# The last batch's gated products in equal 1024-wide pieces, with two two-bank value tiles

## The chip, the core and the metric

The kernel runs on one core of a Trainium2 chip. The metric is the device time of one execution in microseconds. [...] Each engine takes its instructions in the order in which the program lists them, and semaphores order the engines among each other.

## The reference

Per batch an induced attention block (32 inducing vectors attend to 12416 tokens, and the tokens attend to the result), and then a gated feed-forward layer over all tokens:

```python
def mab(q, kv):
    s = scale * (q @ kv.transpose(0, 2, 1))
    s = s - s.max(-1, keepdims=True)
    a = np.exp(s)
    a /= a.sum(-1, keepdims=True) + 1e-09
    return a @ kv
h = mab(I, x)            # B=4, m=32, C=128
attn = mab(x, h)         # N=12416 tokens a batch
...
gate = 1.0 / (1.0 + np.exp(-(x @ w_gate)))   # x: 49664 x 128, w_gate: 128 x 1536
val = x @ w_val
return (gate * val @ w_out).astype(np.float32)
```

## The kernel before

Four batches follow each other; a batch has 97 chunks of 128 tokens, and six groups of 16 chunks plus one chunk left over. Since the second attention's output is a (weights, 32 wide) times h, the kernel folds h into the two weight matrices (`hwt`), so that the feed-forward layer multiplies the 32-wide transposed attention weights `a2r` by `hwt` directly. Hidden columns come in 12 strips of 128 (`NJ`), tokens in blocks of four chunks, 512 tokens (`BC`). There are 97 blocks, the last of them made of the four leftover chunks.

The main loop goes through *steps*. Before, a block has eight: strips are taken two, one, two, one and so on, and a step of two strips is 1024 wide, a step of one 512. `product(t)` (L1033) puts on PE the value matmuls of step t into `v_ps` and the gate matmuls of step t + 2 into `g_ps` (both by `hidden_mm`, L998), and on DVE the product u = (t + 1) * v (L1042). `gate(t)` (L1023) puts the tanh that empties `g_ps` into an SBUF tile on ACT (L1029); the sigmoid is a half of 1 + tanh of a half. `project` (L1063) puts the projections on PE (L1073): four 128 x 128 matmuls a strip, which add u times w_out into the one-bank tile `acc`; after a block's last strip ACT copies `acc` out (L1091) and SP stores it. In the very last block the result stands in two tiles, of which ACT copies one and DVE the other (L1084, L1086).

PSUM's eight banks before: gate tiles of two banks and of one (`g2`, `g1`), value tiles of two banks and of one (`v2`, `v1`), `acc` one, and `m` one for everything else. Each is a single buffer, so a refill of a gate tile waits for the tanh that reads it, and a refill of a value tile for the product that reads it. Before, a wide product also waits, by a dependency added by hand, for the gate refill of step t + 2.

The attention of other groups is worked in between. A *slot* is two steps of the loop; `at(slot, make, late)` plans a piece, and `beside` issues it after the product of that slot's first or second step. `plan_stage2` plans a group's second attention: two slots of score matmuls into `m` (L609), a copy of the scores to SBUF by ACT (L643), lowering by the row maximum on POOL, exp on ACT (L669), sums, inverse and spreading on POOL, and a transposing DMA on SP that makes `a2r`. In the last batch, whose first slot is called o here (slot 288, step 576), groups 2 to 5 are scored from slots o + 4, o + 20, o + 36 and o + 56 on; the scores lie in one SBUF buffer, `sc`. Slot 12 of the last batch, o + 12, begins with step 600 and block 75; 22 blocks follow from there, with block 96.

The order around the change is the order in which this code is written: no scheduler moves an instruction, and `project` is called at the end of every second step, with room for three or four strips.

Of the kernel before, what the change touches and what calls it, by code (L numbers as in the profile page):

```python
# [19 lines left out]
BC = 4  # L20
# [6 lines left out]
def kernel(  # L27
# [34 lines left out]

    ps = ctx.enter_context(tc.tile_pool(name="ps", bufs=1, space=bass.MemoryType.PSUM))

    xv = x.rearrange("b (p j) c -> b p j c", p=P)
    ov = out.rearrange("(b p j) c -> b p j c", b=B, p=P)
# [19 lines left out]
    def x_transpose_dma(b, s):  # L88
        c0, n = groups[s]
        if s == 0 and b > 1:  # L90
            c0, n = 0, n + NLO
        xT_tile(b)
        nc.sync.dma_start(
            xT[b][:, c0 : c0 + n, :],
            xn[b][:, c0 : c0 + n, :].rearrange("p j c -> p (j c)"),
            transpose=True,
        )

    xT_tile(0)
    idle = xT[0][:, NCH - 4 : NCH, :]  # L100
# [614 lines left out]
        for j in range(n):  # L715
            a2[(b, c + j)] = (a2r, j)

    def plan_stage2(b, c, score, take, weigh, far=None, soon=False, lag=None):
# [6 lines left out]
        def room():  # L725
            st["sc"] = s2p.tile([P, GC + NLO, m], F32, tag="sc", name="sc", bufs=1)
# [36 lines left out]
        if far is not None:  # L763
            at(far, one)
            at(far + 1, lambda: s2_take(st["sc"], GC, NLO, st["s2"]))
        at(score, lambda: half(0, False))
        at(score + 1, lambda: half(GC // 2, not soon))
        if soon:
            for k in range(2):
                at(weigh - 1 + k, lambda k=k: s2_shift(GC, st["s2"], *st["hl"], which=(k,)))  # L770
        else:
            at(take, keep, late=True)
            at(take if lag is None else lag, lower, late=lag is None)
# [218 lines left out]
    for i in range(len(blocks)):  # L992
        for j in range(0, NJ, 3):
            steps.append(dict(block=i, j0=j, cnt=2))
            steps.append(dict(block=i, j0=j + 2, cnt=1))
    NST = len(steps)

    def hidden_mm(st, what, halves=False):  # L998
        pt = ps.tile([P, st["cnt"], 512], F32, tag=f"{what}{st['cnt']}", name=f"{what}_ps")
        pieces, col = [], 0  # L1000
        for b, c, nb in blocks[st["block"]]:
            pieces += [(k, b, c, nb, col) for k in range(st["cnt"])]
            col += nb * P
        if not halves:
            pieces.sort(key=lambda p: p[0])
        for k, b, c, nb, col in pieces:
            j = st["j0"] + k
            r = 32 * (j % 2 + (2 if what == "v" else 0))
            a2r, o = a2[(b, c)]
            st[what + "end"] = nc.tensor.matmul(  # L1010
                pt[:, k, col : col + nb * P],
                hw[b][r : r + 32, j // 2, :],
                a2r[r : r + 32, o : o + nb, :].rearrange("p j t -> p (j t)"),
                start=True,
                stop=True,
            )
        st[what] = pt

    def gate_fill(t):
        if t < NST:  # L1020
            hidden_mm(steps[t], "g", t == 0)

    def gate(t):  # L1023
        if t < NST:
            st = steps[t]
            st["t"] = tp.tile([P, st["cnt"], 512], F16, tag=f"t{st['cnt']}", name="t16")
            cuts = [0, 512] if t else [0, 256, 512]
            for c, e in zip(cuts, cuts[1:]):
                st["tanh"] = nc.scalar.activation(  # L1029
                    out=st["t"][:, :, c:e], in_=st["g"][:, :, c:e], func=AF.Tanh, scale=0.5  # L1030
                )

    def product(t):  # L1033
        st = steps[t]
        hidden_mm(st, "v")
        if t == 0:
            keep_on(3, "acc")
        gate_fill(t + 2)
        st["u"] = up.tile([P, st["cnt"], 512], F16, tag=f"u{st['cnt']}", name="u16")
        cuts = [0, 512] if 0 < t < NST - 1 else [0, 256, 512]  # L1040
        for c, e in zip(cuts, cuts[1:]):
            u = nc.vector.scalar_tensor_tensor(  # L1042
                out=st["u"][:, :, c:e],
                in0=st["t"][:, :, c:e],
                scalar=1.0,
                in1=st["v"][:, :, c:e],
                op0=ALU.add,
                op1=ALU.mult,
            )
            if t == 0 and c == 0:  # L1050
                turn_b()
        if st["cnt"] == 2 and 4 <= t < NST - 2:

            tc.declare_no_dep(u.ins, st["tanh"].ins, reason="the gate fill of t + 2 waits for it")
            tc.add_manual_dep(
                u.ins, steps[t + 2]["gend"].ins.name, AFTER, reason="tanh, gate fill, product"
            )

    acc = [None]
# [3 lines left out]
    def project(upto, now, room):  # L1063
        while queue and queue[-1][0] < upto and room > 0:
            t, k = queue.pop()
            st = steps[t]
            j = st["j0"] + k
            if j == 0:
                acc[0] = [ps.tile([P, BC, C], F32, tag="acc", name="acc_ps")]
                if st["block"] == len(blocks) - 1:  # L1070
                    acc[0].append(ps.tile([P, BC, C], F32, tag="m", name="acc_ps"))
            for i in range(BC):
                nc.tensor.matmul(  # L1073
                    acc[0][(i // 2) % len(acc[0])][:, i, :],
                    st["u"][:, k, ts(i, P)],
                    wo16[:, NI * (j % 2) + j // 2, :],
                    start=(j == 0 and i in ((0, 2) if len(acc[0]) > 1 else (0,))),
                    stop=(j == NJ - 1),
                    skip_group_check=True,
                )  # L1080
            room -= 1
            if t == NST - 1:
                o32 = op.tile([P, BC, C], F32, tag="o32")
                nc.scalar.mul(out=o32[:, 0:2], in_=acc[0][0][:, 0:2], mul=0.5)  # L1084
                nc.scalar.dma_start(ov0[:, 0, 0:2, :], o32[:, 0:2])
                nc.vector.tensor_scalar_mul(out=o32[:, 2:4], in0=acc[0][1][:, 2:4], scalar1=0.5)  # L1086
                nc.sync.dma_start(ov0[:, 0, 2:4, :], o32[:, 2:4])
            elif j == NJ - 1:
                block = blocks[st["block"]]
                o32 = op.tile([P, BC, C], F32, tag="o32")  # L1090
                nc.scalar.mul(out=o32[:], in_=acc[0][0][:], mul=0.5)  # L1091
                b, c, nb = block[0]
                nc.sync.dma_start(ov[b, :, c : c + BC, :], o32[:])
                if now < NST:
                    return


    base = [first_step[(b, 0)] // 2 for b in range(B)]
    for b in range(B):
# [6 lines left out]
        for s in range(3 if b == 0 else 2, NG - 1):  # L1106
            k = o + 16 * s - 28
            if b == 0 and s == 4:
                k += 1
                plan_stage2(b, groups[s][0], k, k + 1, k + 13)  # L1110
                continue
            lag = k + 4 if b and more and s == 3 else None
            plan_stage2(b, groups[s][0], k, k + 2, k + (14 if more else 10), lag=lag)
        late = 2 if more and b else 0
        plan_stage2(b, groups[NG - 1][0], o + 56, o + 58, o + 66, far=o + 52 + late)
        if not more:
            continue
        if b == 0:
            parts = {
                2: (23, (29, 29, 29)),  # L1120
# [55 lines left out]
    for t in range(2):  # L1176
        gate_fill(t)
        gate(t)
    for t in range(NST):
        product(t)  # L1180
        gate(t + 2)
        if t % 2 == 0:
# [1 line left out]
        else:  # L1184
            beside(t // 2, True)
            project(t - 1, t, 3 if waiting(t - 1) <= 3 else 4)
    assert not plan
    project(NST, NST, 10**6)

# [29 lines left out]
```

## Time and profile before

| what | before |
|---|---|
| median of 3 runs | 717.21 us (717.18 to 717.42) |
| the profiled execution | 717.26 us |
| its span, first to last instruction | 715.3 us |
| granted TensorE clock in it | 0.999 |
| DVE busy in the span | 697.8 us (98%) |
| ACT busy | 674.2 us (94%) |
| PE busy | 648.1 us (91%) |
| POOL busy | 446.6 us (62%) |

The table's busy times are unions of records. On DVE, ACT and PE a record of one instruction overlaps the start of the next, so that a busy share near 100% doesn't say by itself that no more instructions would fit; what an instruction costs its engine is the distance from its start to the next one's. In a timeline row, the first number is the start in us from the span's start, the second the length that the row covers, "x12" the number of instructions merged into it, and a bracket the idle time before it and what released it.

### The profile page before, as it was taken

What the parts mean: (1) busy time and instruction counts of PE and PEld (TensorE: products, weight loads), DVE (VectorE), ACT (ScalarE), POOL (GpSimd) and SP (SyncE); (2) the same over time, 40 slices, a digit from 0 to 9 for tenths busy, and PEclk for the clock granted to TensorE, in tenths of its full rate; (3) what the DMA queues carried; (4) which work ended last, traced back from release to release, by engine and by line L of the source; (5) the groups of instructions that cost most, each with busy time, mean ns of one, the idle gap of its engine ahead of it and who ended that gap; (6) DMA issues with size and microseconds to landing.
All of it is one profiled execution on the core that took longest, in us unless ns stands there. A gap on an engine that the chain in (4) does not pass through costs nothing.

```text
span 715.3 us, 21657 instructions
## 1 busy us (share of the span) xinstructions
PE 648.1 (91%) x8475; PEld 393.2 (55%) x8475; DVE 697.8 (98%) x850; ACT 674.2 (94%) x1018; POOL 446.6 (62%) x780
## 2 busy tenths in 40 slices
PE   7999899998999999999998989999989889898887
PEld 4555465555555555655555556555555555555555
DVE  4899999999999999999999999999999999999997
ACT  4799999999999999999999999999999999999996
POOL 4468863887558978668656887587737546535100
PEclk9999999999999999999999999999999999999999
DMA  8979964254583264155484142221222123121201
GB/s 172 178 132 187 139 134 92 75 119 88 110 164 75 67 118 108 58 116 108 92 158 106 49 76 77 60 61 51 57 76 64 42 75 61 45 60 46 76 32 47
DMA packets 116855, 65.24 MB, mean 91 GB/s; under 512 B 99952, under 2 KB 101136, under 8 KB 116752
## 3 DMA queue, kind: packets, MB, share of 16 engines
q1 hardware_dynamic: 112064, 49.83, 31.4%
q0 software_dynamic: 4416, 13.90, 10.9%
q8 instruction: 66, 1.08, 0.6%
q14 instruction: 37, 0.30, 0.1%
q10 hardware_dynamic: 272, 0.13, 0.1%
HBM read 27.80 MB, written 25.43 MB: 74 GB/s over the span
## 4 chain that ended last, share of the span: by engine, by line
DVE 49%; issue 20%; PE 16%; ACT 11%; DMA 2%; DVEq 1%; POOL 0%; ACTq 0%; POOLq 0%
DVE u L1042 47%; ACT t L1029 10%; PE acc_ps L1073 7%; PE v_ps L1010 6%; DMA xn<-in_x_dram 2%; PE hp_ps L281 1%; DVE nm L233 1%; DVEq L1042 1%; PE g_ps L1010 1%; POOL xn L82 0%; ACT a1T L246 0%; ACT hwt L468 0%; PE s_ps L609 0%; DVE nmx L620 0%; ACT o L1091 0%
## 5 line engine op out<-in xcount | busy, mean ns | idle before, releaser
L1042 DVE SCALAR_TENSOR_TENSOR u<-t,v_ps 128x512 f16<-128x512 f16 (+1 forms) x778 | 674.9, 945 | 1.1 <-ACT t L1029 0.6
L1029 ACT ACTIVATE t<-g_ps 128x512 f16<-128x512 f32 (+1 forms) x777 | 592.3, 820 | 20.6 <-ACT t L1029 12.7
L1010 PE MATMUL v_ps<-a2r,hwt 32*128 32x512 f16 (+1 forms) x1188 | 293.9, 371 | 55.3 <-DVE u L1042 53.9
L1073 PE MATMUL acc_ps<-wo,u 128*128 128x128 f16 x4656 | 327.6, 220 | 0.2
L1073 PEld LDWEIGHTS <-u 128*128 128x128 f16 x4656 | 261.0, 98 | 88.4 <-issue 87.5
L1010 PE MATMUL g_ps<-a2r,hwt 32*128 32x512 f16 (+1 forms) x1188 | 297.0, 377 | 0.0
L1010 PEld LDWEIGHTS <-hwt 32*128 32x128 f16 x2424 | 92.7, 91 | 185.8 <-issue 140.4
L699 POOL TENSOR_TENSOR a2n<-e,rs 128x2048 f16<-128x2048 f16 (+3 forms) x25 | 86.8, 3474 | 5.0 <-DVE rs L688 2.1
L677 POOL TENSOR_TENSOR sum<-e 128x256 f32<-128x256 f16 (+1 forms) x23 | 15.4, 669 | 97.6 <-ACT e L669 97.6
L438 POOL TENSOR_TENSOR near<-sme,minus 128x16 f32<-128x16 f32 (+1 forms) x22 | 65.2, 2963 | 1.6
L1091 ACT ACTIVATE o<-acc_ps 128x512 f32<-128x512 f32 x96 | 58.2, 607 | 0.0
L653 POOL TENSOR_TENSOR rise<-sc 128x256 f32<-128x256 f32 (+1 forms) x22 | 16.3, 739 | 43.4 <-ACT sc L643 43.3
L654 POOL TENSOR_SCALAR rise<-rise 128x256 f32<-128x256 f32 (+6 forms) x110 | 30.1, 273 | 9.6
L657 POOL TENSOR_TENSOR top<-top,rise 128x128 f32<-128x128 f32 (+3 forms) x88 | 28.3, 321 | 7.3
L677 POOL TENSOR_TENSOR sum<-sum 128x128 f32<-128x128 f32 (+3 forms) x92 | 28.3, 308 | 7.2
L653 POOL TENSOR_TENSOR rise<-top 128x128 f32<-128x128 f32 (+3 forms) x88 | 27.2, 309 | 6.9
L660 POOL TENSOR_TENSOR sc<-sc,top 128x512 f32<-128x512 f32 (+1 forms) x22 | 23.9, 1086 | 1.7
L609 PEld LDWEIGHTS <-xT 128*128 128x128 f16 x388 | 13.1, 96 | 11.7 <-issue 11.3
L82 POOL DMA_DIRECT2D xn<-in_x_dram x25 | 14.9, 602 | 6.5 <-DMA xn<-in_x_dram 5.6
L609 PE MATMUL s_ps<-hT,xT 128*128 128x32 f16 x388 | 18.2, 178 | 0.1
L657 POOL TENSOR_TENSOR top<-sc,rise 128x256 f32<-128x256 f32 (+1 forms) x22 | 16.2, 737 | 1.8
L360 POOL TENSOR_TENSOR xT<-xT 128x512 f32<-128x512 f32 (+2 forms) x13 | 12.4, 954 | 4.2 <-ACT xT L343 3.6
(160 smaller groups left out, 282.4 us busy)
## 6 DMA issues: line engine op xcount, KB each, us to landing
out_dram<-o SPq DMA_DIRECT2D x96, 256.0 KB, 2.3
xn<-in_x_dram POOLq DMA_DIRECT2D x19, 512.0 KB, 8.0
xn<-in_x_dram POOLq DMA_DIRECT2D x4, 544.0 KB, 6.4
a2r<-a2n SPq DMA_TRANSPOSE x29, 4.4
xn<-in_x_dram POOLq DMA_DIRECT2D x1, 384.0 KB, 14.8
wg<-in_moe_w_gate_dram POOLq DMA_DIRECT2D x1, 384.0 KB, 16.3
wv<-in_moe_w_val_dram POOLq DMA_DIRECT2D x1, 384.0 KB, 16.6
wo<-in_moe_w_out_dram POOLq DMA_DIRECT2D x1, 384.0 KB, 16.1
```

The costliest lines, as they stand in the source:

```text
L438: nc.gpsimd.tensor_tensor(out=near, in0=x, in1=minus, op=ALU.pow)
L609: nc.tensor.matmul(s2[:, j, :], xT[b][:, c + j, :], hT16[b][:], start=(j == 0), stop=whole and j == j1 - 1, skip_group_check=True,)
L653: nc.gpsimd.tensor_tensor(out=r, in0=far, in1=near, op=ALU.subtract)
L654: nc.gpsimd.tensor_scalar(out=r, in0=r, scalar1=BIG, scalar2=0.0, op0=ALU.min, op1=ALU.max)
L657: nc.gpsimd.tensor_tensor(out=top[:, 0:n, 0:w], in0=near, in1=r, op=ALU.add)
L677: nc.gpsimd.tensor_tensor(out=d[:, 0:n, :], in0=src[:, :, 0:w], in1=src[:, :, w : 2 * w], op=ALU.add)
L699: eng.tensor_tensor(out=a2n[:, 0:n, :, :], in0=e.unsqueeze(2).to_broadcast((P, n, 4, m)), in1=rs.unsqueeze(2).unsqueeze(3).to_broadcast((P ...
L1010: st[what + "end"] = nc.tensor.matmul(pt[:, k, col : col + nb * P], hw[b][r : r + 32, j // 2, :], a2r[r : r + 32, o : o + nb, :].rearrange ...
L1029: st["tanh"] = nc.scalar.activation(out=st["t"][:, :, c:e], in_=st["g"][:, :, c:e], func=AF.Tanh, scale=0.5)
L1042: u = nc.vector.scalar_tensor_tensor(out=st["u"][:, :, c:e], in0=st["t"][:, :, c:e], scalar=1.0, in1=st["v"][:, :, c:e], op0=ALU.add, op1= ...
L1073: nc.tensor.matmul(acc[0][(i // 2) % len(acc[0])][:, i, :], st["u"][:, k, ts(i, P)], wo16[:, NI * (j % 2) + j // 2, :], start=(j == 0 and ...
L1091: nc.scalar.mul(out=o32[:], in_=acc[0][0][:], mul=0.5)
```

## The change

Up to slot 12 of the last batch the loop keeps its steps. From there on:

- Every product is 1024 wide: a block has six steps of two strips. The gates are still made in eight pieces of two strips and one (`gates`), six strips and four pieces to three steps.
- PSUM is laid out anew: the pool with `v1` and `m` is closed, and its two banks become a second two-bank value tile `vw`; value refills take `v2` and `vw` in turn.
- The tanh results go to the space of batch 2's token tile `xn[2]`, four sets of six strips, since a product now reads strips that two tanh instructions made.
- `project` runs after every step, with room for two or three strips, and not in the step after a block's copy.
- `m` is gone there, so the last batch's scores are made ahead, from slots o - 8, o, o + 4 and o + 8 on, and copied aside into batch 2's transposed token tile `xT[2]`. Lowering, exp and the rest keep their slots.
- The very last block has one `acc` tile; its last product is cut at 384 of 512 tokens, and its last eight projections are ordered to match.
- Apart from the region: eight transposing DMAs of token groups (batches 2 and 3, groups 1 to 4) are issued in two pieces of eight chunks.

```diff
+    gates = steps
+    T0 = first_step[(B - 1, 0)] + 2 * 12
+    steps = gates[:T0]
+    for i in range(gates[T0]["block"], len(blocks)):
+        for j in range(0, NJ, 2):
+            steps.append(dict(block=i, j0=j, cnt=2, bank="vw" if j % 4 else "v2"))
...
     def product(t):
...
-        gate_fill(t + 2)
+        if t < T0:
+            gate_fill(t + 2)
+        else:
+            st["t"] = wide_t((t - T0) // 3, st["j0"], 2)
+            k = T0 + (t - T0) // 3 * 4
+            gate_fill(k + (2, 3, 4)[(t - T0) % 3])
...
-        cuts = [0, 512] if 0 < t < NST - 1 else [0, 256, 512]
+        cuts = [0, 256, 512] if t == 0 else [0, 512] if t < NST - 1 else [0, 384, 512]
...
-        if st["cnt"] == 2 and 4 <= t < NST - 2:
+        if st["cnt"] == 2 and 4 <= t < T0:
...
+            todo = [(k, i) for i in range(BC)]
+            if t == NST - 1:
+                k, _ = queue.pop()[1], None
+                j = st["j0"] + k
+                todo = [(n, i) for n in range(2) for i in range(BC - 1)] + [(n, BC - 1) for n in range(2)]
...
-                nc.scalar.mul(out=o32[:, 0:2], in_=acc[0][0][:, 0:2], mul=0.5)
+                nc.scalar.mul(out=o32[:, 0:2], in_=acc[0][:, 0:2], mul=0.5)
...
-                nc.vector.tensor_scalar_mul(out=o32[:, 2:4], in0=acc[0][1][:, 2:4], scalar1=0.5)
+                nc.vector.tensor_scalar_mul(out=o32[:, 2:4], in0=acc[0][:, 2:4], scalar1=0.5)
...
+            if not more:
+                early = o + 4 * (s - 2) - (8 if s == 2 else 4)
+                plan_stage2(b, groups[s][0], early, early + 2, k + 10, low=k + 2)
+                continue
...
+            plan_stage2(b, groups[NG - 1][0], o + 8, o + 10, o + 66, far=o - 4, low=o + 58)
...
-    for t in range(NST):
+    for t in range(T0):
...
+    narrow.close()
+    ps.open(ctx, "psw", "vw")
+    stored = False
+    for t in range(T0, NST):
+        six, part = divmod(t - T0, 3)
+        product(t)
+        gate(T0 + 4 * six + 2 + part)
+        if part == 2:
+            gate_fill(T0 + 4 * six + 5)
+            gate(T0 + 4 * six + 5)
+        for slot, late in ([(0, False)], [(0, True), (1, False)], [(1, True)])[part]:
+            beside(T0 // 2 + 2 * six + slot, late)
+        if stored:
+            stored = False
+        else:
+            stored = project(t - 1, t, 2 if waiting(t - 1) <= 2 else 3)
```

Two places of the built order. First PE in the middle of the region, before: the refills of a wide and a narrow step, and the projections (`acc_ps`) behind them (weight loads, and rows like the one above them, left out).

```order
L1010 MATMUL v_ps<-a2r,hwt 128x512 [waits DVE_49]
...
L1010 MATMUL g_ps<-a2r,hwt 128x512 [waits Activation_49]
...
L1010 MATMUL v_ps<-a2r,hwt 128x512 [waits DVE_49]
...
L1010 MATMUL g_ps<-a2r,hwt 128x512 [waits Activation_49]
...
L1073 MATMUL acc_ps<-wo_109,u_13221 128x128 [waits Activation_49]
...
L1073 MATMUL acc_ps<-wo_109,u_13229 128x128
```

Twelve projections (three strips) stand behind the narrow step's refills, and the next wide refill stands behind them. PE at the same place after the change, from a block's sixth pass to the third pass of the next:

```order
L1042 MATMUL v_ps<-a2r,hwt 128x512 [waits DVE_49]
...
L1042 MATMUL g_ps<-a2r,hwt 128x512 [waits Activation_49]
...
L1042 MATMUL v_ps<-a2r,hwt 128x512 [waits DVE_49]
...
L1042 MATMUL g_ps<-a2r,hwt 128x512 [waits Activation_49]
...
L1122 MATMUL acc_ps<-wo_112,u_13150 128x128
...
L1122 MATMUL acc_ps<-wo_112,u_13166 128x128
...
L1042 MATMUL v_ps<-a2r,hwt 128x512 [waits DVE_49]
...
L1042 MATMUL g_ps<-a2r,hwt 128x512 [waits Activation_49]
...
L1122 MATMUL acc_ps<-wo_112,u_13186 128x128
```

The first two rows are the sixth pass, with no projection behind its refills; then the first pass has 12 projections (eight of u_13150, four of u_13166), and the second pass 12 again (four of u_13166, eight of u_13186). The projections that stood behind one narrow gate refill now stand behind a wide one and the next narrow one.

Second, ACT over a block after the change (`xn` is where tanh writes, `o` the copy of a finished block):

```order
L1140 ACTIVATE o_13769<-acc_ps 128x512
L1069 ACTIVATE xn_1758<-g_ps 128x1024
L1069 ACTIVATE xn_1758<-g_ps 128x512
L1069 ACTIVATE xn_1758<-g_ps 128x1024
L1069 ACTIVATE xn_1758<-g_ps 128x512
L1069 ACTIVATE xn_1758<-g_ps 128x1024
L1069 ACTIVATE xn_1758<-g_ps 128x512
L1069 ACTIVATE xn_1758<-g_ps 128x1024
L1069 ACTIVATE xn_1758<-g_ps 128x512
L1140 ACTIVATE o_13879<-acc_ps 128x512
```

Between two copies stand the same eight tanh instructions as before; the copy stands behind a narrow tanh and ahead of a wide one. At the program's end DVE's last rows are, before:

```order
L1042 SCALAR_TENSOR_TENSOR u_15208<-t_15171,v_ps 128x1024 [waits PE_49,Activation_49]
L1042 SCALAR_TENSOR_TENSOR u_15215<-t_15185,v_ps 128x256 [waits PE_49,Activation_49]
L1042 SCALAR_TENSOR_TENSOR u_15215<-t_15185,v_ps 128x256
L1086 TENSOR_SCALAR o_15242<-acc_ps 128x256 [waits DMAHW4_49,DMAHW3_49,DMAHW5_49,DMAHW2_49,DMAHW6_49,DMAHW1_49,DMAHW7_49,DMAHW0_49,PE_49]
L1214 UNCONDITIONAL_BRANCH
```

and after:

```order
L1087 SCALAR_TENSOR_TENSOR u_14893<-xn_1758,v_ps 128x1024 [waits DVE_49,PE_49,Activation_49]
L1087 SCALAR_TENSOR_TENSOR u_14917<-xn_1758,v_ps 128x2x384 [waits DVE_49,PE_49,Activation_49]
L1087 SCALAR_TENSOR_TENSOR u_14917<-xn_1758,v_ps 128x2x128
L1135 TENSOR_SCALAR o_14944<-acc_ps 128x256 [waits DMAHW4_49,DMAHW3_49,DMAHW5_49,DMAHW2_49,DMAHW6_49,DMAHW1_49,DMAHW7_49,DMAHW0_49,Activation_49]
L1285 UNCONDITIONAL_BRANCH
```

DVE's last copy now waits for ACT's copy out of the same tile, where it waited for PE before.

More of the change, by code (lines that the diff above doesn't have):

```diff
@@ L92, in x_transpose_dma @@
         xT_tile(b)
[L93 to L97, printed above, removed]
+        cuts = [c0, c0 + GC // 2, c0 + n] if b > 1 and 0 < s < NG - 1 else [c0, c0 + n]
+        for c, e in zip(cuts, cuts[1:]):
+            nc.sync.dma_start(
+                xT[b][:, c:e, :],
+                xn[b][:, c:e, :].rearrange("p j c -> p (j c)"),
+                transpose=True,
+            )
     xT_tile(0)
@@ L772, in plan_stage2 @@
             at(take, keep, late=True)
-            at(take if lag is None else lag, lower, late=lag is None)
+            at(low or take if lag is None else lag, lower, late=lag is None)
         at(weigh, exp, late=True)
@@ L1051, in product @@
                 turn_b()
-        if st["cnt"] == 2 and 4 <= t < NST - 2:
+        if st["cnt"] == 2 and 4 <= t < T0:
             tc.declare_no_dep(u.ins, st["tanh"].ins, reason="the gate fill of t + 2 waits for it")
             tc.add_manual_dep(
-                u.ins, steps[t + 2]["gend"].ins.name, AFTER, reason="tanh, gate fill, product"
+                u.ins, gates[t + 2]["gend"].ins.name, AFTER, reason="tanh, gate fill, product"
             )
@@ L1068, in project @@
             if j == 0:
[L1069 to L1078, printed above, removed]
+                acc[0] = ps.tile([P, BC, C], F32, tag="acc", name="acc_ps")
+            todo = [(k, i) for i in range(BC)]
[3 more added lines that the diff above has]
+                todo = [(n, i) for n in range(2) for i in range(BC - 1)] + [(n, BC - 1) for n in range(2)]
+            for n, i in todo:
+                e = st["j0"] + n
+                nc.tensor.matmul(
+                    acc[0][:, i, :],
+                    st["u"][:, n, ts(i, P)],
+                    wo16[:, NI * (e % 2) + e // 2, :],
+                    start=(e == 0 and i == 0),
+                    stop=(e == NJ - 1),
                     skip_group_check=True,
```

59 lines of the change are left out of this document (44 added, 15 removed).

## The prediction

> **What bounds the kernel now.** I read the page first: its span, the chain that ended last, and the costliest groups.
>
> ```profile
> span 715.3 us, 21657 instructions
> DVE 49%; issue 20%; PE 16%; ACT 11%; DMA 2%; DVEq 1%; POOL 0%; ACTq 0%; POOLq 0%
> L1042 DVE SCALAR_TENSOR_TENSOR u<-t,v_ps 128x1024 f16<-128x1024 f16 x387 | 470.1, 1215 | 0.3
> L1042 DVE SCALAR_TENSOR_TENSOR u<-t,v_ps 128x512 f16<-128x512 f16 x389 | 264.5, 680 | 0.8 <-ACT t L1029 0.6 <-PE g_ps L1010 0.3
> ```
>
> The products on DVE (L1042) carry the chain, and their idle time is about 1 us in 715. But 470.1 + 264.5 is 734.6 us, more than the span: the records overlap, so a recorded duration is not what one more product costs. That is the distance between starts. Here is DVE's timeline at four neighbouring starts (start, length of the row, count):
>
> ```profile
> 640.77 1.81 DVE L1042 SCALAR_TENSOR_TENSOR u<-t,v_ps 128x512 f16<-128x512 f16 x2
> 641.37 1.81 DVE L1042 SCALAR_TENSOR_TENSOR u<-t,v_ps 128x1024 f16<-128x1024 f16 x2
> 642.50 1.81 DVE L1042 SCALAR_TENSOR_TENSOR u<-t,v_ps 128x512 f16<-128x512 f16 x2
> 643.10 1.81 DVE L1042 SCALAR_TENSOR_TENSOR u<-t,v_ps 128x1024 f16<-128x1024 f16 x2
> ```
>
> A narrow product takes 0.60 us from start to start, a wide one 1.13, a pair 1.73, and a block of four pairs 6.92. A wide one is 0.07 cheaper than two narrow ones. Two refills of matmuls on PE stand behind each pair; their timeline, and the tanh (L1029) that one of them feeds:
>
> ```profile
> 644.36 0.39 PE L1010 MATMUL v_ps<-a2r,hwt 32*128 32x512 f16 x2
> 644.37 0.39 PE L1010 MATMUL g_ps<-a2r,hwt 32*128 32x512 f16 x2
> 644.96 0.37 PE L1010 MATMUL v_ps<-a2r,hwt 32*128 32x512 f16 x1 [0.20 <-DVE u L1042]
> 644.97 0.38 PE L1010 MATMUL g_ps<-a2r,hwt 32*128 32x512 f16 x1
> 645.28 0.84 PE L1073 MATMUL acc_ps<-wo,u 128*128 128x128 f16 x12
> 646.09 0.39 PE L1010 MATMUL v_ps<-a2r,hwt 32*128 32x512 f16 x2
> 646.59 1.02 ACT L1029 ACTIVATE t<-g_ps 128x1024 f16<-128x1024 f32 x1 [0.22 <-ACT t L1029]
> ```
>
> Value and gate refills start 0.01 apart and run side by side. PE waits for DVE here (0.20), and ACT waits too (0.22), so DVE's own rate sets the pace.
>
> **The change, part by part.** The region runs from the first product of slot 12 of the last batch to the last product:
>
> ```profile
> L1042 DVE SCALAR_TENSOR_TENSOR u<-t,v_ps x177: 412/681/1223, 558.1 to 710.6; 128x1024 f16<-128x1024 f16 x88, 128x512 f16<-128x512 f16 x87, 128x256 f16<-128x256 f16 x2
> ```
>
> That is 176 steps (one split in two), 22 blocks, 558.1 to 711.0 (the last record takes 0.41): 152.9 us. The change makes 132 wide products of them, 6 x 1.13 = 6.78 a block instead of 6.92. **On DVE alone** that saves 22 x 0.14 = 3.0 us. The question is whether PE and ACT can feed a block every 6.78 us.
>
> **The new feeding order.** A block now has six passes on PE: two value matmuls, then the gate refill, then old projections. The gate still comes as wide, narrow, wide, narrow, out of one wide and one narrow buffer, so a gate refill must wait until tanh has emptied the same buffer. In the built order the six passes hold 12, 12, 8, 8, 8 and 0 projections; gate refills are wide, narrow, wide and narrow, wide, narrow, wide and narrow. ACT copies the block out after the fifth pass's narrow tanh, ahead of the sixth pass's wide one. What these steps cost is read where before shows them without slack. First a tanh whose refill waits for it, and whose refill the next tanh waits for:
>
> ```profile
> 605.24 1.06 ACT L1029 ACTIVATE t<-g_ps 128x1024 f16<-128x1024 f32 x1
> 606.16 0.39 PE L1010 MATMUL v_ps<-a2r,hwt 32*128 32x512 f16 x2
> 606.35 0.39 PE L1010 MATMUL g_ps<-a2r,hwt 32*128 32x512 f16 x2
> 606.83 1.02 ACT L1029 ACTIVATE t<-g_ps 128x1024 f16<-128x1024 f32 x1
> 606.75 0.37 PE L1010 MATMUL v_ps<-a2r,hwt 32*128 32x512 f16 x1
> 606.84 0.37 PE L1010 MATMUL g_ps<-a2r,hwt 32*128 32x512 f16 x1
> 607.15 0.23 PE L1073 MATMUL acc_ps<-wo,u 128*128 128x128 f16 x1
> ```
>
> The tanh ends at 606.30, its refill starts 0.05 later, and the next tanh 0.48 after that. The refill stands still at 606.16 to 606.35 while it waits, and so does all that follows on PE: the projections start 0.31 behind the held-up refill at 606.84, not ahead of it. Next a pass of 12 projections that nobody holds up, and ACT's steps back to back:
>
> ```profile
> 490.85 0.39 PE L1010 MATMUL v_ps<-a2r,hwt 32*128 32x512 f16 x1
> 491.17 0.84 PE L1073 MATMUL acc_ps<-wo,u 128*128 128x128 f16 x12
> 491.94 0.39 PE L1010 MATMUL v_ps<-a2r,hwt 32*128 32x512 f16 x2
> 603.38 1.51 ACT L1029 ACTIVATE t<-g_ps 128x1024 f16<-128x1024 f32 x2 [0.33 <-ACT t L1029]
> 604.30 0.59 ACT L1029 ACTIVATE t<-g_ps 128x512 f16<-128x512 f32 x1
> 642.32 0.59 ACT L1029 ACTIVATE t<-g_ps 128x512 f16<-128x512 f32 x1
> 642.79 0.60 ACT L1091 ACTIVATE o<-acc_ps 128x512 f32<-128x512 f32 x1
> 643.27 1.05 ACT L1029 ACTIVATE t<-g_ps 128x1024 f16<-128x1024 f32 x1
> ```
>
> The pass takes 491.94 - 490.85 = 1.09 from refill to refill. From start to start ACT takes 0.92 for a wide tanh, 0.47 for a narrow one, 0.48 for a copy.
>
> **The cycle.** Now follow one block from the wide tanh of a sixth pass.
> (1) It takes 1.05, plus 0.05 to the wide refill of the next first pass, which waits for it: 1.10.
> (2) Behind that refill stand 12 projections: 1.09 to the second pass.
> (3) The second pass has 12 more: 1.10 with the 0.01 between value and gate.
> (4) The third pass's wide refill, free to start, feeds its tanh: 0.01 + 0.48 = 0.49.
> (5) That tanh alone takes 1.02, plus 0.05 to the fourth pass's wide refill, which waits for it: 1.07.
> (6) Refill to tanh: 0.48.
> (7) Wide tanh, 0.92; (8) narrow tanh of the fifth pass, 0.47; (9) the block's copy, 0.48; and the next sixth-pass tanh begins.
> Sum: 1.10 + 1.09 + 1.10 + 0.49 + 1.07 + 0.48 + 0.92 + 0.47 + 0.48 = **7.20 us a block**. DVE is nowhere in it. The products need 6.78, so they will wait about 0.42 a block, for the tanh of (7). Value refills are not late: a product's buffer is free 1.21 + 0.05 after its start, half a microsecond before PE comes to it. In the old order the two tight places cannot add up, since 12 projections follow only a narrow gate refill, and the wide one comes next with 0.2 in hand.
>
> **Sum.** The first block still lives on what is ahead (6.78); 21 blocks take 7.20; the split last product adds 0.07 and its record's overhang 0.08: 6.78 + 151.2 + 0.15 = 158.1, against 152.9, so +5.2.
>
> **The end.** These are ACT's, DVE's and SP's last instructions before:
>
> ```profile
> 711.16 0.38 ACT L1084 ACTIVATE o<-acc_ps 128x256 f32<-128x256 f32 x1 [2.28 <-PE acc_ps L1073]
> 711.38 0.42 DVE L1086 TENSOR_SCALAR o<-acc_ps 128x256 f32<-128x256 f32 x1 [0.38 <-PE acc_ps L1073]
> 711.83 0.40 SPq L1087 DMA_DIRECT2D out_dram<-o  x1
> ```
>
> Two accumulator tiles let both copies run at once. With one tile ACT's copy waits for the last projection, so it starts near 711.38, and DVE's copy now waits for ACT's: 0.38 + 0.06 later. That is +0.45 on the path.
>
> **Smaller parts.** The last batch's four score copies (0.48 each on ACT) move to before slot 12, where ACT spends 1.39 of each 1.73; where such a copy stood before, the products slipped by at most 0.24 (from 604.21 to 604.88 is 0.67 for 0.60, from there to 606.78 is 1.90 for 1.73):
>
> ```profile
> 604.21 1.90 DVE L1042 SCALAR_TENSOR_TENSOR u<-t,v_ps 128x512 f16<-128x512 f16 x2
> 604.88 1.82 DVE L1042 SCALAR_TENSOR_TENSOR u<-t,v_ps 128x1024 f16<-128x1024 f16 x2
> 606.78 1.22 DVE L1042 SCALAR_TENSOR_TENSOR u<-t,v_ps 128x1024 f16<-128x1024 f16 x1
> ```
>
> So -0.24 to +0.96; I take 0. PE's 16 small score matmuls and POOL's work keep their lengths, and softmax still has eight slots between lowering and exp. Eight transpositions more on SP's queue:
>
> ```profile
> a2r<-a2n SPq DMA_TRANSPOSE x29, 4.4
> 602.11 3.38 SPq L710 DMA_TRANSPOSE a2r<-a2n  x1
> ```
>
> One holds the queue for 3.38 us, and output stores are queued behind it, three copies deep, at 6.9 us a block. Cut pieces should hold it for about the same in all; if each cost a full one more, stores would still fit. 0, from -0.5 to +0.5. Without the old rule "product after gate refill" a product can only start sooner: 0.
>
> Against the profiled execution, 717.26 (span 715.3 and 1.96 around it; 0.05 above the median of the runs), the sum is +5.2 + 0.45: **722.9 us**.
>
> [...]
>
> **Rivals.**
> *A, products stay the bound: faster.* If PE runs the 12 projections of the first pass while its gate refill still waits, link (2) loses the 0.62 from first to last of them and 0.1 of switching. The cycle is then 6.48, under 6.78, and only DVE counts: -3.0, up to -0.5 for old stalls gone, +0.45: about 714.6. It decides below a cycle of 6.93, where 21 c + 6.78 + 0.15 + 0.45 is 152.9. For it speaks that weight loads already overlap matmuls; against it the projection at 607.15. The Trainium skill (TensorE: Matmul & The Clock Gate, section The mechanism, and the one on the array's architectural detail) has matmuls in strict order and only LDWEIGHTS pulled ahead; that row agrees, and by the order rule 7.20 stands.
> *B, the cycle holds but is shorter.* Ten hand-overs 0.025 quicker than at the places I read give 6.95, and 717.7: no change.
> *C, wide products in a row cost more.* Before, a wide one always stood between narrow ones. Were each to take its record of 1.21, the region would take 132 x 1.21 + 0.07 = 159.8: 724.6. Against it: the overlap is 0.08 after both forms.
>
> **Numbers.** Forecast 0.70, A 0.14, B 0.09, C 0.07. A cycle read to +-0.1 gives 720.8 to 725.0; with the scores' bound 725.5. The range takes in B and leaves out A: 716.4 to 725.5. A measurement of this kernel tells 0.2% (1.4 us) from no change: faster 0.15 (A and an edge of B), same 0.06, slower 0.79.
>
> **What would show it.** Right: the distance of output copies in the region is near 7.2; DVE idles before products, released by tanh; PE waits at gate refills for tanh and no longer at value refills for DVE; at the end DVE's copy starts after ACT's ends. Wrong: DVE stays gapless with starts 1.13 apart (A), or 1.21 apart (C).

## The result, and the profile after

The changed kernel is slower: 723.34 us, median of four runs (721.86, 723.29, 723.39, 724.47), against 717.19 for the kernel before (717.11 to 717.42, four runs). The ratio is 1.0084, with a 95% interval of 1.0072 to 1.0097. The forecast was 722.9, with a range of 716.4 to 725.5.

In the rows PE is TensorE, DVE VectorE, ACT ScalarE, POOL GpSimd and SP SyncE. The page's span, its chain and its groups of products, as shown of before:

```profile
span 722.5 us, 21536 instructions
ACT 1%; DVE 1%; issue 0%; PE 0%; ACTq 0%
L1087 DVE SCALAR_TENSOR_TENSOR u<-t,v_ps 128x512 f16<-128x512 f16 x601 | 522.2, 946 | 1.0 <-ACT t L1069 0.5
L1087 DVE SCALAR_TENSOR_TENSOR u<-xn,v_ps 128x1024 f16<-128x1024 f16 (+1 forms) x133 | 153.3, 1209 | 4.4 <-ACT xn L1069 3.6
```

The chain of waits breaks off here after about 2% of the span, so it says nothing about the region. The groups do: 601 products ahead of the region wait 1.0 us in all, the 133 of the region 4.4, most of it for tanh (`xn` is where tanh now writes). DVE's timeline (start, length of the row, count, idle time before) shows that the waits are regular:

```profile
619.11 7.01 DVE L1087 SCALAR_TENSOR_TENSOR u<-xn,v_ps 128x1024 f16<-128x1024 f16 x6 [0.16 <-ACT xn L1069]
626.28 7.01 DVE L1087 SCALAR_TENSOR_TENSOR u<-xn,v_ps 128x1024 f16<-128x1024 f16 x6 [0.16 <-ACT xn L1069]
633.45 1.22 DVE L1087 SCALAR_TENSOR_TENSOR u<-xn,v_ps 128x1024 f16<-128x1024 f16 x1 [0.16 <-ACT xn L1069]
```

Six products, one block, take 7.17 us from start to start. Six at 1.131 would take 6.79. The starts have three distances: 1.13 to 1.14 without a wait, 1.38 ahead of one product of a block, and 1.25 ahead of another, which the row of six hides. The timeline of PE, and then of ACT, over one block:

```profile
627.55 0.39 PE L1042 MATMUL v_ps<-a2r,hwt 32*128 32x512 f16 x2 [0.40 <-DVE u L1087]
628.22 0.39 PE L1042 MATMUL g_ps<-a2r,hwt 32*128 32x512 f16 x2 [0.27 <-ACT xn L1069]
628.54 0.84 PE L1122 MATMUL acc_ps<-wo,u 128*128 128x128 f16 x12
629.32 0.39 PE L1042 MATMUL v_ps<-a2r,hwt 32*128 32x512 f16 x2
...
629.64 0.84 PE L1122 MATMUL acc_ps<-wo,u 128*128 128x128 f16 x12
...
630.42 0.60 PE L1042 MATMUL g_ps<-a2r,hwt 32*128 32x512 f16 x3
...
631.96 0.39 PE L1042 MATMUL g_ps<-a2r,hwt 32*128 32x512 f16 x2
```

```profile
625.22 1.51 ACT L1069 ACTIVATE xn<-g_ps 128x1024 f16<-128x1024 f32 x2
626.65 0.60 ACT L1140 ACTIVATE o<-acc_ps 128x512 f32<-128x512 f32 x1
627.15 3.23 ACT L1069 ACTIVATE xn<-g_ps 128x1024 f16<-128x1024 f32 x4
630.89 3.02 ACT L1069 ACTIVATE xn<-g_ps 128x1024 f16<-128x1024 f32 x4 [0.51 <-PE g_ps L1042]
632.39 1.02 ACT L1069 ACTIVATE xn<-g_ps 128x1024 f16<-128x1024 f32 x1
633.31 0.59 ACT L1069 ACTIVATE xn<-g_ps 128x512 f16<-128x512 f32 x1
633.82 0.60 ACT L1140 ACTIVATE o<-acc_ps 128x512 f32<-128x512 f32 x1
634.31 1.02 ACT L1069 ACTIVATE xn<-g_ps 128x1024 f16<-128x1024 f32 x1
```

The rows at 632.39 and 633.31 are the last two of the four tanh instructions merged above them. The cycle can be read from these rows alone. The sixth pass's wide tanh starts at 627.15, its buffer's next refill at 628.22 (1.07). Twelve projections bring PE to the second pass at 629.32 (1.10), twelve more to the third at 630.42 (1.10). The tanh there starts at 630.89 (0.47), and the fourth pass's refill of the same buffer at 631.96 (1.07). From there the wide tanh follows at 632.39 (0.43), then the narrow one at 633.31 (0.92), the copy at 633.82 (0.51), and the next sixth-pass tanh at 634.31 (0.49). The sum is 7.16, and output copies stand 633.82 - 626.65 = 7.17 apart.

From its first to its last product the region lasts 718.43 - 560.76 = 157.67 us, against 152.88 before: **+4.79**. From the first product of the program to the region it takes 527.94, against 527.89 before. At the end, ACT's and DVE's copies and the last store:

```profile
718.81 0.38 ACT L1133 ACTIVATE o<-acc_ps 128x256 f32<-128x256 f32 x1 [2.14 <-PE acc_ps L1122]
719.23 0.42 DVE L1135 TENSOR_SCALAR o<-acc_ps 128x256 f32<-128x256 f32 x1 [0.80 <-ACT o L1133]
719.68 0.39 SPq L1136 DMA_DIRECT2D out_dram<-o  x1
```

DVE's copy waits 0.80 instead of 0.38, for ACT's. But from the issue of the last store to the span's end only 2.8 us pass, where it was 3.4 before (715.26 - 711.83). So from the last product's end to the end of the span it is 4.08, against 4.26 before: **-0.18**.

The profiled execution (724.47) lost 2.6 us more, and at the start. Windows of the first microseconds, of after and then of before (window, its length, busy time of PE, weight loads, DVE, ACT and POOL with instruction counts, granted clock, DMA share, GB/s):

```profile
16.00:18.00 2.00, 0.13 (x1) 0.00 (x0) 1.03 (x4) 1.48 (x5) 0.00 (x0) 1.00 1.05 204
18.00:20.00 2.00, 1.64 (x20) 1.32 (x20) 0.13 (x1) 0.13 (x1) 1.24 (x7) 0.71 1.14 215
20.00:22.00 2.00, 2.00 (x30) 0.98 (x27) 1.21 (x3) 1.62 (x4) 1.75 (x4) 0.50 1.07 209
22.00:24.00 2.00, 1.76 (x22) 1.21 (x20) 1.97 (x4) 1.30 (x5) 1.06 (x2) 0.93 1.25 201
```

```profile
16.00:18.00 2.00, 1.44 (x22) 1.03 (x21) 1.24 (x5) 1.69 (x6) 0.90 (x5) 1.00 1.06 207
18.00:20.00 2.00, 1.87 (x39) 1.20 (x36) 1.80 (x3) 1.62 (x4) 1.76 (x6) 1.00 1.13 210
```

And the matmul in after's timeline that ends the gap, with the same matmul in the profiled execution of run 4 below it (the change without output copies, described in the next section):

```profile
18.36 1.47 PE L808 MATMUL xt_ps<-ident,xn 128*128 128x128 f16 x16 [2.23 <-DMA xn<-in_x_dram]
18.24 1.07 PE L808 MATMUL xt_ps<-ident,xn 128*128 128x128 f16 x16 [2.17 <-DMA xn<-in_x_dram]
```

PE stands empty for 2.23 us, waiting for a load of x, and then runs at a granted clock of 0.5; the first product starts at 32.82 instead of 30.23. In run 4 nearly the same gap is followed by the full clock, and the first product starts at 31.59; that execution took 721.11, the other two 719.74 and 719.76. So a late load alone costs some 1.4 us there, and load and half clock together 2.6 here. The kernel before has runs as far above its others too (718.7 to 719.8 among 717.2), of which there is no profile. Without the late start the change costs 4.79 - 0.18 + 0.05 = 4.66, and 717.19 + 4.66 is 721.85: the fastest run is 721.86.

### The profile page after: what moved, and what is told of

It is laid out like the page before. It is cut to its first block, busy times and chain, and to the rows that moved or that the text cites. A ratio compares the mean times of both kernels' runs of the same rounds, so it can differ in the third digit from the quotient of the medians.

```text
span 722.5 us, 21536 instructions
## 1 busy us (share of the span) xinstructions
PE 654.2 (91%) x8475; PEld 392.6 (54%) x8475; DVE 698.3 (97%) x806; ACT 677.1 (94%) x1018; POOL 446.4 (62%) x780
## 5 line engine op out<-in xcount | busy, mean ns | idle before, releaser
L1087 DVE SCALAR_TENSOR_TENSOR u<-t,v_ps 128x512 f16<-128x512 f16 x601 | 522.2, 946 | 1.0 <-ACT t L1069 0.5
L1069 ACT ACTIVATE t<-g_ps 128x512 f16<-128x512 f32 x601 | 458.7, 821 | 11.5 <-ACT t L1069 4.7
L1122 PE MATMUL acc_ps<-wo,u 128*128 128x128 f16 x4656 | 331.1, 220 | 0.2
L1042 PE MATMUL v_ps<-a2r,hwt 32*128 32x512 f16 (+1 forms) x1188 | 277.7, 373 | 46.9 <-DVE u L1087 45.7
L1042 PE MATMUL g_ps<-a2r,hwt 32*128 32x512 f16 (+1 forms) x1188 | 289.4, 376 | 7.4 <-ACT xn L1069 6.0
L1087 DVE SCALAR_TENSOR_TENSOR u<-xn,v_ps 128x1024 f16<-128x1024 f16 (+1 forms) x133 | 153.3, 1209 | 4.4 <-ACT xn L1069 3.6
L1069 ACT ACTIVATE xn<-g_ps 128x1024 f16<-128x1024 f32 (+1 forms) x176 | 135.1, 810 | 11.4 <-PE g_ps L1042 9.0
L668 POOL TENSOR_TENSOR rise<-sc 128x256 f32<-128x256 f32 (+1 forms) x18 | 13.3, 738 | 21.6 <-ACT sc L658 21.5
L675 POOL TENSOR_TENSOR sc<-sc,top 128x512 f32<-128x512 f32 (+1 forms) x18 | 19.5, 1084 | 1.4
```

Source lines behind the costliest of these rows:

```text
L668: nc.gpsimd.tensor_tensor(out=r, in0=far, in1=near, op=ALU.subtract)
L1042: st[what + "end"] = nc.tensor.matmul(pt[:, k, col : col + nb * P], hw[b][r : r + 32, j // 2, :], a2r[r : r + 32, o : o + nb, :].rearrange ...
L1069: st["tanh"] = nc.scalar.activation(out=st["t"][:, :, c:e], in_=st["g"][:, :, c:e], func=AF.Tanh, scale=0.5)
L1087: u = nc.vector.scalar_tensor_tensor(out=st["u"][:, :, c:e], in0=st["t"][:, :, c:e], scalar=1.0, in1=st["v"][:, :, c:e], op0=ALU.add, op1= ...
L1122: nc.tensor.matmul(acc[0][:, i, :], st["u"][:, n, ts(i, P)], wo16[:, NI * (e % 2) + e // 2, :], start=(e == 0 and i == 0), stop=(e == NJ - 1),
```

## The experiments

The theory is the cycle: what counts is how many projections stand on the path from tanh to refill to tanh. Two rivals stand against it in the first four runs: R1, wide products or their waits cost more in themselves; R2, ACT's own work is the bound. Region lengths are from the region's first product to the end of the last.

**1. Projections ahead of the held-up gate refill** (in a block's first and fourth passes):

```diff
-    def product(t):
+    def product(t, between=None):
         hidden_mm(st, "v")
+        if between is not None:
+            between()
         ...
-        product(t)
+        product(t, old if part == 0 else None)
```

> Edit: in the 22 blocks, passes that refill a wide gate alone issue their old projections between the value refill and the gate refill, so that the projections run while the refill waits for tanh. Theory (a cycle through PE's order and ACT of 7.17 us a block, in which projections stand behind a refill that waits): the 1.09 us of the first link and the second such place leave the cycle, DVE's 6.79 is left, the region falls from 157.7 to about 149.5 us, starts of products are 1.13 apart nearly everywhere; 713.7 to 714.5 us, about 3 us faster than before the change. Rival R1 (wide products or their waits on DVE cost more): still 7.17 a block, 157.7. Rival R2 (ACT's own work is the bound): still 7.17.

Measured: 732.64 us (732.11 to 733.66, four runs), ratio 1.0216 (1.02 to 1.0231), region 168.26. This missed. Its PE, and DVE's products:

```profile
622.02 0.39 PE L1042 MATMUL v_ps<-a2r,hwt 32*128 32x512 f16 x2 [0.40 <-DVE u L1089]
622.34 0.84 PE L1124 MATMUL acc_ps<-wo,u 128*128 128x128 f16 x12
623.12 0.39 PE L1042 MATMUL g_ps<-a2r,hwt 32*128 32x512 f16 x2
```

```profile
620.74 3.48 DVE L1089 SCALAR_TENSOR_TENSOR u<-xn,v_ps 128x1024 f16<-128x1024 f16 x3 [0.24 <-ACT xn L1069]
624.60 3.48 DVE L1089 SCALAR_TENSOR_TENSOR u<-xn,v_ps 128x1024 f16<-128x1024 f16 x3 [0.38 <-ACT xn L1069]
```

The value refill waits for the product that began at 620.74 (1.28 to 622.02). Behind it come 12 projections (1.10), then the gate refill; its tanh starts 0.43 later, and the product that reads it 1.05 after that: 3.86 for three products that need 3.39. The block's other half, with 8 projections in that place, takes 3.72, so a block takes 7.58 instead of 7.17. The edit took one link out and put DVE's product into a new cycle with the same projections in it. The gate refill was late before because of tanh; now it is late because of a value refill that had cost nothing as long as nothing urgent stood behind it.

**2. Eight projections in every pass, none left out:**

```diff
-        if stored:
-            stored = False
-        else:
-            stored = project(t - 1, t, 2 if waiting(t - 1) <= 2 else 3)
+        project(t - 1, t, 2 if waiting(t - 1) <= 2 else 3)
```

> Edit: every pass gets 8 projections (two strips), none is left out after a copy, so the passes hold 8, 8, 8, 8, 8, 8 and the sixth waits for the copy of the finished block. Theory: links (2) and (3) lose 4 x 0.056 us each, 7.17 becomes 6.72, below DVE's 6.79: region about 150 us, 714 to 715 us. R1 and R2: no change, 157.7.

Measured: 713.81 us (713.69 to 713.87, four runs), ratio 0.9951 (0.9936 to 0.9966), region 149.48. DVE in the middle of the region:

```profile
611.32 29.50 DVE L1087 SCALAR_TENSOR_TENSOR u<-xn,v_ps 128x1024 f16<-128x1024 f16 x26
```

Twenty-six products without a wait: (29.50 - 1.21) / 25 = 1.13 from start to start, and 132 x 1.131 + 0.15 is 149.4. The products, tiles, tanh pieces and copies are those of the change; only the places of the same projections differ. So wide products in a row don't cost more, and ACT can feed them: R1 and R2 fall. This version is faster than both kernels.

**3. One pass of 12** (12, 8, 8, 8, 8, 4):

```diff
-    stored = False
+    since = 2
...
+        room = (1, 3, 2)[min(since, 2)]
+        since = 0 if project(t - 1, t, room) else since + 1
```

> Edit: as the even one, but the sixth pass has 4 projections and the next block's first pass 12; the second pass has 8. Theory: only link (3) loses 0.22 us, the cycle is 6.94, halfway between: region about 153 us, some 717 to 718 us. R1 and R2: no change, 157.7. If the even one is DVE bound and this one too (149.5), the cycle is shorter elsewhere than I think.

Measured: 717.77 us (717.65 to 717.92, ten runs), ratio 1.0004 (0.9994 to 1.0013), region 153.48; output copies mostly 6.94 apart. With one of the two passes of 12, 4.2 of the 8.2 us are gone by which the change's region exceeds run 2's. Before this change the products took the same 6.92 a block, so the gain and the loss cancel here.

**4. No output copies** after the region's first two blocks (all later blocks but the last are neither copied nor stored):

```diff
-                o32 = op.tile([P, BC, C], F32, tag="o32")
-                nc.scalar.mul(out=o32[:], in_=acc[0][:], mul=0.5)
+                if now <= T0 + 12 or now >= NST:
+                    ...
```

> Edit: the copies and stores of the finished blocks after the first two of the region are left out (those outputs aren't written). Theory: the wide tanh behind the copy can start only 0.10 us sooner, when its refill lands, so 7.07 a block, region about 155.7 us. R2 (ACT bound): 0.48 us a block less, down to DVE's 6.79, region about 150. R1: no change, 157.7.

Measured: 719.76 us (719.74, 719.76, 721.11), ratio 1.004 (1.0024 to 1.0056), region 155.28. ACT has 0.5 us less to do in each block, yet a block still takes 7.05:

```profile
617.22 6.88 DVE L1087 SCALAR_TENSOR_TENSOR u<-xn,v_ps 128x1024 f16<-128x1024 f16 x6 [0.16 <-ACT xn L1069]
624.26 6.89 DVE L1087 SCALAR_TENSOR_TENSOR u<-xn,v_ps 128x1024 f16<-128x1024 f16 x6 [0.16 <-ACT xn L1069]
```

ACT's own work is not the bound.

**5. The kernel before with early scores and cut transpositions alone**, the steps, tiles and end as before:

```diff
...
+        cuts = [c0, c0 + GC // 2, c0 + n] if b > 1 and 0 < s < NG - 1 else [c0, c0 + n]
...
+                plan_stage2(b, groups[s][0], early, early + 2, k + 10, low=k + 2)
```

> The kernel before, with only two parts of the change: the last batch's scores made ahead and copied aside, and eight transpositions in two pieces; the steps, the tiles and the end stay as before. Theory (the loss comes from the region's feeding cycle alone): 717.2 us, 716.9 to 717.6, from the first product to the product that opens slot 12 of the last batch 527.9 us, and from there to the last product's end 152.9. Rival (the moved copies or the pieces cost a part of the loss): 718 to 720 us, with the distance to slot 12 longer than 528.2.

Measured: 716.77 us (716.65 to 716.91, ten runs), ratio 0.9987 (0.9978 to 0.9996). To slot 12 it is 527.95, the region 152.64, and the tail behind it 4.00 instead of 4.26. The loss is not here. The two parts together even gain a little, which the expectation had not allowed for: 0.24 in the region, from which the score copies have gone, and 0.26 behind the last product, whose cause these runs don't show.

**6. The change again**, with nothing edited, for its spread:

> The kernel after once more, for the spread of its runs. Theory (a late load of x delays the start in some executions of any kernel by 1.4 to 2.6 us, and has nothing to do with the change): the fastest runs lie at 721.8 to 722.0 us, others 1.4 to 2.6 above them, and some runs of the kernel before show the same step; in the profiled execution the region lasts 157.7 us, whatever the first product's start. Rival (the region itself varies): region lengths between 156 and 159, with the first product at the same time as before (30.2).

Measured: 721.82, 721.87, 721.91, 723.27, 724.22 us; ratio 1.0067 (1.0049 to 1.0085). In its profiled execution the first product starts at 30.23, as before, and the region lasts 157.66, as in the execution with the late start. So the region is the same in both, and some 721.9 is the change's time when nothing delays the start.

**7. The passes of 12 moved** behind the third and fourth passes' gate refills (8, 8, 12, 12, 8, 0):

```diff
-    stored = False
+    since = 1
...
+        room = (0, 2, 2, 3, 3, 2)[min(since, 5)]
+        since = 0 if project(t - 1, t, room) else since + 1
```

> The change with its passes of 8, 8, 12, 12, 8 and 0 projections in place of 12, 12, 8, 8, 8 and 0: as many passes of 12 and the same pass left out, but the passes of 12 stand behind the third and fourth passes' gate refills, where PE waits for tanh in the kernel after. Theory (it is where the 12 stand in the cycle that counts): the cycle falls by two times 0.31 to about 6.59 us a block, below the products' 6.78, so VectorE sets the pace: region 149.5 to 150.3 us, time 713.7 to 714.8. Rival (unevenness itself costs, a pass of 12 or a pass without projections each stalling VectorE wherever it stands): 7.1 to 7.2 us a block, region 156 to 158, time 720 to 722.

Measured: 717.68 us (717.53 to 719.03, ten runs), ratio 1.0003 (0.9992 to 1.0013), region 153.35, a block 6.94: neither the theory's number nor the rival's. Its PE from a first pass's gate refill to the fifth pass's, and ACT:

```profile
637.84 0.39 PE L1042 MATMUL g_ps<-a2r,hwt 32*128 32x512 f16 x2 [0.39 <-ACT xn L1069]
638.16 0.62 PE L1122 MATMUL acc_ps<-wo,u 128*128 128x128 f16 x8
638.72 0.39 PE L1042 MATMUL v_ps<-a2r,hwt 32*128 32x512 f16 x2
...
639.60 0.60 PE L1042 MATMUL g_ps<-a2r,hwt 32*128 32x512 f16 x3
640.13 0.84 PE L1122 MATMUL acc_ps<-wo,u 128*128 128x128 f16 x12
...
641.14 0.39 PE L1042 MATMUL g_ps<-a2r,hwt 32*128 32x512 f16 x2
641.47 0.84 PE L1122 MATMUL acc_ps<-wo,u 128*128 128x128 f16 x12
...
642.25 0.38 PE L1042 MATMUL g_ps<-a2r,hwt 32*128 32x512 f16 x1
```

```profile
636.77 3.01 ACT L1069 ACTIVATE xn<-g_ps 128x1024 f16<-128x1024 f32 x4
640.07 3.24 ACT L1069 ACTIVATE xn<-g_ps 128x1024 f16<-128x1024 f32 x4 [0.29 <-PE g_ps L1042]
643.22 0.60 ACT L1140 ACTIVATE o<-acc_ps 128x512 f32<-128x512 f32 x1
643.72 1.51 ACT L1069 ACTIVATE xn<-g_ps 128x1024 f16<-128x1024 f32 x2
```

A pass of 8 takes 0.88 (637.84 to 638.72), so four projections are worth 0.22, at 0.055 each, not the 0.31 that the expectation took. And the fourth pass has too little slack. Its 12 projections bring the fifth pass's narrow refill to 642.25, 1.11 behind the fourth's; its tanh, 0.46 later, has overtaken the wide one as what ACT waits for. The links now sum to 1.07 + 0.88 + 0.88 + 0.47 + 1.07 + 1.11 + 0.46 + 0.51 + 0.49 = 6.94. That left two readings: the 12 in the fourth pass, or a pass without projections as such.

**8. Sixteen in the third pass** (8, 8, 16, 8, 8, 0), an edit of run 7:

```diff
-        room = (0, 2, 2, 3, 3, 2)[min(since, 5)]
+        room = (0, 2, 2, 4, 2, 2)[min(since, 5)]
```

> The change with passes of 8, 8, 16, 8, 8 and 0 projections. The run with 8, 8, 12, 12, 8 and 0 left open whether the pass without projections costs, or the 12 in its fourth pass; read link by link its cycle was 1.07 + 0.88 + 0.88 + 0.47 + 1.07 + 1.11 + 0.46 + 0.51 + 0.49 = 6.94 us, where the 1.11 is the fourth pass's 12 and a pass of 8 took 0.88. Theory (only projections on the cycle count, and its path through the third pass goes by tanh, 0.47 + 1.07 = 1.54, under which 16 projections fit at about 1.53): the cycle falls to 1.07 + 0.88 + 0.88 + 0.47 + 1.07 + 0.43 + 0.92 + 0.51 + 0.49 = 6.72, below the products' 6.78; VectorE sets the pace, region 149.5 to 150.3 us, time 713.7 to 714.7. Rival (a pass without projections, or uneven passes as such, stall VectorE wherever they stand): 6.94 us a block or more, region 153 us or more, time 717.5 or more.

Measured: 713.7 us median of ten runs (eight of them 713.53 to 713.81, one 715.13, one 719.23), ratio 0.9955 (0.9937 to 0.9972). After its first two waits the region runs at DVE's pace, with the most uneven passes of all and one left out:

```profile
604.79 45.33 DVE L1087 SCALAR_TENSOR_TENSOR u<-xn,v_ps 128x1024 f16<-128x1024 f16 x40
```

(45.33 - 1.21) / 39 is 1.13. The region was 150.92 in this execution, the 715.13 one; 1.44 of it are two long starts near 563 us, at a clock of 0.5 (last section). Without them it is 149.48, as in run 2.

**9. Twelve in the first and the third pass** (12, 8, 12, 8, 8, 0), another:

```diff
-        room = (0, 2, 2, 3, 3, 2)[min(since, 5)]
+        room = (0, 3, 2, 3, 2, 2)[min(since, 5)]
```

> The change with passes of 12, 8, 12, 8, 8 and 0 projections. Theory (by the same links, the first pass's four extra projections add 4 x 0.055 = 0.22 to the cycle and the third pass's four nothing): 6.72 + 0.22 = 6.94 us a block, region 153.0 to 153.8, time 717.2 to 718.1. Rival (each pass of 12 costs the same wherever it stands): as in the kernel after, 7.1 to 7.2 a block, region 156.5 to 158, time 721 to 722.

Measured: 717.74 to 717.8 us in five of ten runs, 718.96 to 721.59 in the others, median 718.38; ratio 1.0018 (1.0004 to 1.0031). The profiled execution (717.8) has a region of 153.48 and copies 6.94 apart, as expected. That is run 3's region too, whose passes differ only in that the third pass's four extra projections stand in the sixth: they cost nothing. By the links the first pass's cost 0.22 (6.72 to 6.94). The median is above what was expected, by five runs that are 1.2 to 3.9 above the others. There is no profile of them, but their granted clock is 0.994 to 0.998, where the other five have 0.999 or 1.0; stretches of half clock, as in the last section, are the likely cause, not a shown one.

## Why the prediction was right, step by step

- **What bounded the kernel before** (products 1.13 and 0.60 apart, PE and ACT waiting for DVE) holds: the same wide products, fed in time, run 1.13 apart in runs 2 and 8. The 3.0 us that DVE alone was to save are there as well: region 149.48 against 152.88, 3.4 less, of which run 5 puts 0.24 down to the moved scores.
- **The cycle** of nine links is what limits the change. Forecast 7.20 a block, measured 7.17. Each link is there; the sizes differ by at most 0.05. The longest were read best (1.10 twice for the passes of 12, 1.07 for tanh to refill); the hand-over in (1) was 0.03 shorter, that from refill to tanh in (6) 0.05 shorter, that from tanh to copy in (8) 0.04 longer. Five runs confirm it by its parts: 0.22 less with one pass of 8 (run 3, run 9), 6.94 by other links (run 7), below DVE's need with both gone (run 2, run 8). Run 4 shows that the copy link is worth only 0.12, since without it PE's refill in the sixth pass is the next to be late.
- **Region sum** +5.2, measured +4.79. The first block indeed runs without a wait (6.81). Twenty blocks of 7.165 instead of 7.20 make -0.7, and two longer waits in the last block (starts 1.45 and 1.39 apart) give 0.2 back.
- **Where the products wait**: forecast 0.42 a block for the tanh of (7); measured 0.24 there, and 0.12 at a second place, which was not foreseen: the product behind the second pass's value refill (629.32), which stands behind the first pass's 12 projections. It adds nothing to the cycle; it splits the same wait.
- **"Value refills are not late"** was wrong at two places. One is the refill just named, which comes 0.12 late for its product. The other is behind the pass without projections, where PE is early and waits 0.40 for DVE (627.55). That wait cost nothing in the change, because the gate refill behind it waits for tanh anyway. But the line that was to show the forecast right, "PE no longer waits at value refills for DVE", failed, and run 1 missed for the same reason.
- **The end** was mis-sized: +0.45 forecast, -0.18 measured. The wait of DVE's copy for ACT's came as forecast (0.80 instead of 0.38), and the last store is issued 1.25 behind the last product's end instead of 0.83, here and in every run with this end. What was not foreseen is that this store is followed by 0.6 less. Run 5, whose end is that of before, has part of this (3.2 instead of 3.4); the cause is open.
- **Scores, cut transpositions, the dropped rule**: taken as 0. Run 5 gives about -0.5 for the first two together, with the region's share (-0.24) at the lower bound that the prediction named for the scores. The dropped rule was not tried by itself.
- **Rivals.** A's condition, projections running past a held-up refill, does not occur: at 628.22 the refill waits for tanh, and the projections start behind it at 628.54. A's time, 714.6, came about when the order was changed (runs 2 and 8), and not when only the projections were put first (run 1). B would have needed 6.95. C is refuted by the starts 1.13 apart.
- **The number.** 717.26 + 4.79 - 0.18 + 0.05 gives 721.9, the change undisturbed: 1.0 under the forecast, 0.4 of it the region and 0.6 the end. The median of the first measurement, 723.34, lies 1.4 above that: three of its four runs are 1.4 to 2.6 above the fastest, the profiled one through its late start, the other two presumably so (no profile of them). No term of the forecast held such a delay. That the median came within 0.5 of 722.9 is luck: the forecast was 1.0 too high for the change itself, and the delay added 1.4. The mechanism was right without it. In the range one sum is off: 725.0 with the scores' bound of 0.96 would be 726.0, not 725.5.

The Trainium skill says in Perfetto Trace Analysis, section Optimizing Scalar/DVE Operations, that larger operations can improve throughput if the engine is saturated. Runs 2 and 8, in which DVE's products follow each other without a wait, agree: 0.5% faster. In the change itself the condition isn't met, since its products wait 0.37 us in every block.

## What to carry to other kernels

When the bound engine's work shrinks, write down the closed path by which the other engines feed it, link by link, and compare its length with the bound engine's new need; busy shares of PE and ACT (91% and 94% here) would not have told a gain of 3.5 us from a loss of 4.7. Work that fills an in-order queue costs nothing behind a refill whose consumer is late anyway, and its full length behind one on that path: the same 48 projections a block gave 713.7, 717.7, 721.9 or 732.6 us by place alone. Before putting filler ahead of a refill that waits, look at what the instruction ahead of the filler waits for, since the filler will inherit that wait.

## What the runs showed of the hardware

TensorE's granted clock can fall to half in the middle of a busy stretch, with one core at work. In run 8, windows of half a microsecond (columns as before):

```profile
561.50:562.00 0.50, 0.50 (x11) 0.40 (x9) 0.50 (x2) 0.50 (x1) 0.00 (x0) 1.00 0.27 103
562.00:562.50 0.50, 0.50 (x5) 0.14 (x6) 0.50 (x1) 0.49 (x1) 0.00 (x0) 0.54 0.00 0
...
565.00:565.50 0.50, 0.50 (x8) 0.50 (x6) 0.28 (x1) 0.50 (x2) 0.42 (x2) 0.54 0.00 0
565.50:566.00 0.50, 0.50 (x11) 0.33 (x8) 0.00 (x0) 0.04 (x1) 0.33 (x3) 1.00 0.00 0
```

The half clock lasts 0.46 + 5 x 0.50 + 0.46 = 3.4 us (the five windows left out show 0.50), with PE busy throughout, and costs the products 1.44. After the late load at the start of the profiled change it lasted 3.4 us as well, by the clocks 0.71, 0.50 and 0.93 of the three windows shown there (1.16 + 2.00 + 0.28), behind 2.23 us without a matmul. The Trainium skill (TensorE: Matmul & The Clock Gate, Part 1) gives a window of 3413 ns for the gate that halves the clock, and the length agrees in both places. The Trainium skill has the clock fall there after an idle window of that length. Here it fell behind a gap of 2.23 us in the change, did not fall behind one of 2.17 in run 4, and fell in run 8 with no gap over 0.48 in the 3.4 us before. So by these runs keeping gaps shorter than the window is no safe bound, and what brought the fall in run 8 stays open.

A gate refill that waits holds up the projections behind it (628.22 and 628.54), as the prediction took it from the row at 607.15. But not all matmuls keep the program's order. In its last block the kernel before issues eight value matmuls and then eight gate matmuls (32*128 in the profile). The third value matmul starts at 706.86, behind the first gate matmul at 706.84, and from there the two kinds start in turns. The projections are 128*128.
